# A new order of all queues, and eight PSUM banks shared by attention and MLP

## The chip, the cores and the metric

The kernel is one launch on one core of a Trainium2 chip. The core has engines that work side by side, each through a queue of its own, in the order in which the program gives it its instructions: TensorE (PE; the loading of its weights is listed as PEld), VectorE (DVE), ScalarE (ACT) and GpSimd (POOL). SyncE (SP) issues the DMA transfers in this kernel. An instruction starts when those before it on its engine are done and everything that it reads is there; until then all behind it on that engine stands too. TensorE writes to PSUM, which has eight banks of 2 KB for each of 128 partitions.

The metric is the time of the whole launch in microseconds (us). Three runs of the kernel before took 535.52, 535.54 and 535.78; the median is 535.54.

## What is computed

A recurrent attention, followed by an MLP with a hard-swish:

```python
state = zeros((B, H, D, D))                     # B, H, S, D = 4, 8, 768, 48
for t in range(S):
    state = alpha[:, :, t, :, None] * state + einsum('bhd,bhe->bhde', k[:, :, t], v[:, :, t])
    y[:, :, t] = einsum('bhd,bhde->bhe', q[:, :, t], state)
x = y.transpose(0, 2, 1, 3).reshape(B * S, H * D)     # 3072 x 384
h = x @ w_in                                          # 3072 x 2048
g = h * clip(h + 3, 0, 6) / 6
out = g @ w_out                                       # 3072 x 384
```

q, k, v and alpha come as 32-bit floats, the two weights as 64-bit floats. [...]

## The kernel before

**Tiling.** The tokens are cut into 24 *chunks* of 128, j = 0 to 23: six to each of the four batches, so chunks 0, 6, 12 and 18 begin with an empty state. Two chunks make a *group* of 256 tokens, g = 0 to 11, for the MLP.

**An order written by hand.** All work is cut into steps. A step is a function of the kernel, and the program is one string of 1788 words, each a step's short name and its numbers with dots between: `sc.3.1.3` is the scores of chunk 3 with PSUM tiles 1 and 3. `run` (L745 to L748) calls them one after the other inside `tc.manual_schedule()` (L750). A step may hold instructions for one engine or for several; each engine gets its instructions in the order of the string, and so does SyncE its DMAs. The string therefore sets the order of every queue at once, and which PSUM tile a step writes. Waits between engines follow from the data.

**Weights: 16 slices** of 768 KB, i = 0 to 7 of `w_in` and 8 to 15 of `w_out`. `w.i` loads a slice. `d1.i` (L186) and `d2.i` (L196) are ScalarE's passes over it, `dx.i` (L191) one more for slices 0, 1, 2 and 4; `d3.i` is VectorE's part, two instructions for those four slices (L203 and L205, a "half-size" weight) and three for the others (L207, L208 and L210, a "whole" one); `d4.i` (L217) is an addition on GpSimd that finishes the slice. A matmul on a slice needs its `d4`.

**Attention, for a chunk j.**
- `la`, `lk`, `lq`, `lv` load alpha, k, q and v (L251 and L262, L272). For the first six chunks alpha, k and q are transposed on TensorE (`ta`, `tk`, `tq`: four transposes each, L282, into one PSUM tile); for later ones on VectorE (L286).
- `ca` (L300) copies alpha's transpose to SBUF on ScalarE. `r` is a scan over the chunk on VectorE (L309) and a reciprocal, the decay; `p` (L320) a second scan, the growth. `k` and `q` (L332) multiply k by the one and q by the other, on VectorE.
- `sc` (L346) makes the scores on TensorE, in two PSUM tiles, `m` (L356) masks them on VectorE, four instructions. `qa.j.b` (L366) copies half of q beside the masked scores on ScalarE.
- k by token: `kb` (TensorE, L374) and `ck` (ScalarE, L378) for the first eight chunks; later `kt` (VectorE, L391), `kw` and `kr`, a way through DRAM.
- the state: `st` (L409) decays it on GpSimd, `sv.j.b` (L419; L415 at a batch's start) copies it beside v on ScalarE, `u` (L429) makes the update on TensorE, `sm.j.b` (L437, L439) adds it to the state on VectorE.
- `ya` and `yb` (L455) are the matmuls of the output of the first and second half of the chunk; `cy` (L464) copies the result to SBUF on ScalarE, as x of the MLP.

**MLP.** Groups 0 and 1 make the first layer with plain matmuls: `f` (L478), 12 matmuls for two of the 16 blocks of 128 hidden units; `fa` and `fb` (L489) do the same for the two chunks of group 0 apart. `fr` (ScalarE, L494) and `fg` (VectorE, L498) are the gate. Group 0 makes the second layer with plain matmuls too (`b`, L516, `bo`, `so`).

From group 2 on the first layer is a fast matrix product with 20 sub-products: `y` (VectorE, L537 to L541) makes sums of the blocks of `w_in` once, `xc.g` makes sums of a group's x, `M.g.i` (L600) is sub-product i, four matmuls, `n` (L606) keeps a result on ScalarE, `o` (L537 to L541) combines results on VectorE, `e` (L494) and `h` (L498) are the gate. From group 1 on the second layer has seven sub-products: `x` (L647) makes sums of `w_out` once, `s` (L647, L664) sums of the hidden units on VectorE, `P.g.i` (L703) is sub-product i, eight matmuls of which the profile has 16 records, `K` (L682) keeps a result on ScalarE, `G` (L719, and L716 on ScalarE) finishes a quarter of the output and `O` (L724) stores it.

**Pads.** `z.m.n` (L532) is n matmuls of the identity into a PSUM tile that nobody reads. The profile has two records for each.

**PSUM.** Two lists of four tiles, each tile one bank: `banks`, tiles t0 to t3, for attention's steps (`ta`, `tk`, `tq`, `kb`, `sc`, `u`, `ya`), and `bank_m`, tiles m0 to m3, for those of the MLP and the pads. A number in a word is an index in its list. A step that writes a tile waits until the last reader of what the tile held is done.

```python
banks = [ps.tile([C, NP * C], FP, tag=f"t{i}", name=f"t{i}_ps") for i in range(4)]        # L222
bank_m = [ps.tile([C, GT * 2], FP, tag=f"m{i}", name=f"m{i}_ps") for i in range(4)]       # L470
```

Of the kernel before, what the change touches and what calls it, by code (L numbers as in the profile page):

```python
# [17 lines left out]
def kernel(  # L18
# [42 lines left out]
    G = 2  # L61
# [161 lines left out]
    banks = [ps.tile([C, NP * C], FP, tag=f"t{i}", name=f"t{i}_ps") for i in range(4)]  # L223
# [246 lines left out]
    bank_m = [ps.tile([C, GT * 2], FP, tag=f"m{i}", name=f"m{i}_ps") for i in range(4)]  # L470

# [278 lines left out]
    with tc.manual_schedule():  # L750
        run("""z.0.5 z.0.3 z.0.1 z.0.8 qa.0.0 w.0 d2.0 d3.0 la.0 ta.0.0 ca.0 r.0 lk.0 tk.0.1 k.0
               z.0.2 p.0 la.1 ta.1.2 lq.0 tq.0.3 ca.1 r.1 lk.1 lv.0.0 sv.0.0 d1.0 kb.0.0 ck.0 z.0.2
               u.0.2.1 sm.0.0 sv.0.1 q.0 qa.0.1 tk.1.0 k.1 p.1 z.0.2 sc.0.2.3 m.0 la.2 ta.2.0 ca.2
               dx.0 w.2 d2.2 kb.1.0 ck.1 lq.1 r.2 sm.0.1 st.1 tq.1.2 q.1 d3.2 z.0.3 d1.2 dx.2 lv.1.1
               u.1.3.1 sv.1.0 sm.1.0 p.2 sm.1.1 sc.1.0.2 m.1 ya.0.3 yb.0 cy.0 lq.2 w.1 d1.1 tq.2.1
               q.2 d4.2 lk.2 tk.2.3 k.2 fa.2.0 d4.0 st.2 sc.2.0.2 d2.1 d3.1 m.2 dx.1 d4.1 qa.1.1
               lk.3 la.3 ta.3.1 ca.3 la.4 fa.0.1 sv.1.1 w.3 r.3 ta.4.3 ca.4 r.4 tk.3.1 k.3 kb.2.0
               qa.1.0 d2.3 ya.1.2 yb.1 cy.1 fa.1.2 lq.3 ck.2 d1.3 p.3 d3.3 lv.2.2 u.2.3.2 sm.2.0
               d4.3 fb.2 tq.3.1 q.3 fb.1 qa.2.0 sm.2.1 sv.2.0 st.3 fr.0.2.0 fg.0.2 lk.4 tk.4.0
               sv.2.1 w.5 d2.5 k.4 d3.5 d1.5 qa.3.0 d4.5 qa.2.1 sc.3.1.3 m.3 w.6 d2.6 d1.6 d3.6 d4.6  # L760
               lv.3.0 lq.4 w.7 kb.3.2 fb.0 f.0.3.3 kb.4.0 ya.2.1 ck.3 u.3.3.2 sm.3.0 fr.0.3.1 fg.0.3
               fr.0.1.0 fg.0.1 qa.3.1 sv.3.0 sm.3.1 p.4 d2.7 sv.3.1 d1.7 d3.7 d4.7 f.0.5.0 fr.0.5.1
               fr.0.0.0 fg.0.5 fg.0.0 tq.4.3 ck.4 la.5 ta.5.2 f.0.6.3 ca.5 w.4 d2.4 ya.3.0 yb.3 cy.3
               fr.0.6.1 yb.2 cy.2 w.9 d2.9 q.4 qa.4.1 d1.4 d1.9 dx.4 la.6 w.8 d3.4 r.5 lk.5 w.10
               d3.9 p.5 ca.6 fg.0.6 d4.9 w.12 lq.5 lv.4.1 d2.8 d3.8 f.0.7.2 d1.8 st.4 d4.8 d4.4 w.11
               fr.0.7.0 fg.0.7 f.1.7.0 fr.1.7.1 fg.1.7 sc.4.0.2 m.4 f.1.1.1 fr.1.1.0 fg.1.1 f.1.3.3
               fr.1.3.1 d2.10 d1.10 tk.5.3 f.1.0.2 d2.12 d3.10 d4.10 w.13 fg.1.3 fr.1.0.0 fg.1.0 k.5
               d3.12 lq.6 f.1.6.0 f.1.2.1 u.4.1.0 sm.4.0 d1.12 d4.12 sv.4.0 qa.4.0 ya.4.2 fr.1.6.1
               fg.1.6 w.15 tq.5.3 fa.4.3 sv.4.1 d2.11 kb.5.1 d2.13 fr.1.2.0 f.1.4.2 fr.1.4.1 d1.11
               sm.4.1 q.5 r.6 d3.11 d3.13 fg.1.4 d4.11 lv.5.0 lk.6 tq.6 p.6 d2.15 d3.15 fg.1.2 d1.13  # L770
               d4.13 sc.5.0.3 yb.4 f.1.5.0 fr.1.5.1 fg.1.5 tk.6 m.5 b.1.0.2 fb.4 b.1.1 d1.15 d4.15
               st.5 y.5 w.14 la.7 lk.7 cy.4 d2.14 qa.5.1 ck.5 b.0.0.1 fr.0.4.0 d3.14 k.6 q.6 ca.7
               fg.0.4 d1.14 d4.14 x.0 y.1 y.10 b.0.1 y.0 y.2 u.5.2 P.1.0.0 K.1.0 qa.5.0 sv.5.0
               qa.6.1 P.1.1.3 b.0.2 b.1.2 kb.6.0 ya.5.3 y.6 s.1.0.0 sm.5.0 sv.5.1 G.1.0.0 tk.7
               s.1.1.1 s.1.2.3 x.1 yb.5 cy.5 b.1.3 sc.6.1.2 lv.6.2 ck.6 u.6.3.0 s.1.3.2 x.2 P.1.2
               b.0.3 K.1.1 y.7 s.1.4 s.1.5 y.11 y.3 r.7 xc.2.1 x.3 y.4 y.8 xc.2.3 k.7 xc.2.0 xc.2.4
               y.9 y.12 y.16 y.13 y.15 P.1.3.3 K.1.2 P.1.4 bo.1 P.1.5 xc.2.5 G.1.1.1 P.1.6 y.14 y.17
               y.19 xc.2.6 sm.6.0 G.1.2.2 y.20 M.2.0.2 lv.12.1 la.8 O.1.1 O.1.0 ca.8 y.18 y.21 y.23
               so.1 G.1.3.3 n.2.0.8 bo.0 lq.7 lv.7.0 O.1.2 m.6 xc.2.2 xc.2.10 xc.2.7 tq.7 r.8 p.7
               xc.2.8 sv.6.1 M.2.15.3 M.2.1 kb.7.3 n.2.1.9 M.2.16 M.2.2 n.2.2.10 M.2.7.0 n.2.7.11  # L780
               sm.6.1 xc.2.9 q.7 p.8 M.2.3 M.2.4 n.2.4.12 M.2.8 o.2.0.0 M.2.5 n.2.5.13 qa.7.0 sv.6.0
               st.7 lk.8 O.1.3 lq.8 lk.9 la.9 la.10 tk.8 tq.8 lq.10 lq.9 ya.6.1 yb.6 M.2.9 z.1.3
               M.2.18.1 o.2.1.0 e.2.1.1 M.2.10 cy.6 ck.7 sc.7.0.2 u.7.1.3 n.2.10.14 M.2.11 qa.7.1
               ca.9 la.11 y.22 M.2.6.2 h.2.1 q.8 m.7 e.2.0.0 h.2.0 n.2.11.15 qa.6.0 n.2.18.10 qa.8.1
               M.2.12 M.2.19 n.2.12.12 M.2.13 sm.7.0 sv.7.1 r.9 k.8 o.2.3.0 sv.7.0 ya.7.0 y.24
               o.2.5.0 n.2.13.12 o.2.2.0 yb.7 cy.7 sc.8.1.2 xc.3.1 o.2.2.1 e.2.2.1 xc.3.3 o.2.3.1
               M.2.14 xc.3.4 xc.3.0 xc.3.5 o.2.4.0 xc.3.7 xc.3.6 o.2.6.0 P.2.0.1 M.3.0.2 M.2.17
               h.2.2 o.2.6.1 e.2.3.0 h.2.3 o.2.7.0 K.2.0 n.3.0.12 M.3.1 n.3.1.9 e.2.5.1 M.3.7.0
               n.3.7.13 xc.3.8 o.2.7.1 xc.3.2 kt.8 e.2.6.0 h.2.6 tk.9 M.3.2 n.3.2.10 e.2.4.0 P.2.1.3
               h.2.4 h.2.5 s.2.0.14 e.2.7.0 G.2.0.1 h.2.7 M.3.3 M.3.4 n.3.4.8 k.9 s.2.1.11 M.3.8  # L790
               o.3.0.0 ca.10 kt.9 P.2.3.3 s.2.2.15 s.2.3.14 lv.8.2 kw.8 kr.8 lk.10 sm.7.1 xc.3.9
               M.3.5 n.3.5.11 K.2.2 e.3.0.1 xc.3.10 M.3.9 o.3.1.0 P.2.2 K.2.1 u.8.0.3 M.3.18.2 s.2.5
               M.3.10 n.3.10.14 n.3.18.15 e.3.1.0 s.2.4 P.2.4 tq.9 h.3.0 st.8 sv.8.0 M.3.11 n.3.11.8
               tk.10 p.9 sm.8.0 q.9 r.10 k.10 qa.9.0 qa.9.1 m.8 sm.8.1 h.3.1 M.3.19 o.3.5.0 kt.10
               P.2.5 G.2.2.0 st.9 M.3.12 sc.9.0.1 qa.8.0 n.3.12.10 o.3.3.0 kw.9 lv.9.0 kr.9 sv.8.1
               u.9.2.3 sm.9.0 sv.9.1 sv.9.0 G.2.1.2 sm.9.1 st.10 M.3.15.2 M.3.16 M.3.6.3 M.3.13 m.9
               o.3.4.0 o.3.6.0 tq.10 n.3.13.10 o.3.2.0 e.3.4.1 ya.8.2 yb.8 ya.9.3 yb.9 cy.9 M.3.14
               M.3.17 cy.8 xc.4.1 P.2.6 e.3.5.0 G.2.3.3 o.3.2.1 xc.4.3 h.3.4 xc.4.4 o.3.6.1 xc.4.5
               xc.4.0 xc.4.6 e.3.2.1 M.4.0.0 n.4.0.10 P.3.0.1 xc.4.7 o.3.7.0 p.10 h.3.5 o.3.3.1
               xc.4.8 M.4.7.3 M.4.1 xc.4.2 h.3.2 o.3.7.1 lk.11 O.2.2 tk.11 e.3.6.0 e.3.3.1 h.3.3  # L800
               P.3.1.2 e.3.7.1 n.4.1.13 M.4.2 K.3.0 ca.11 q.10 h.3.6 r.11 k.11 h.3.7 n.4.7.15
               lv.10.2 lv.11.0 kw.10 sc.10.0.1 kr.10 G.3.0.0 u.10.3.2 sm.10.0 qa.10.1 n.4.2.14 M.4.3
               M.4.4 M.4.8 s.3.0.9 xc.4.9 s.3.2.12 s.3.1.11 P.3.3.2 n.4.4.8 M.4.5 o.4.0.0 e.4.0.0
               sv.10.1 sm.10.1 xc.4.10 kt.11 O.2.0 O.2.3 lq.11 m.10 s.3.3.9 s.3.5 M.4.9 o.4.1.0
               P.3.2 sv.10.0 st.11 n.4.5.11 K.3.2 la.13 M.4.18.0 p.11 tq.11 lk.12 tk.12 K.3.1 M.4.10
               n.4.10.9 q.11 qa.10.0 n.4.18.12 e.4.1.1 la.12 s.3.4 ca.12 h.4.0 r.12 P.3.5 G.3.2.1
               h.4.1 M.4.11 P.3.4 n.4.11.8 M.4.12 n.4.12.14 qa.11.0 M.4.19 p.12 G.3.1.3 lq.12 kw.11
               O.2.1 tq.12 kr.11 u.11.3 sc.11.0.2 sv.11.0 O.3.1 lk.13 P.3.6 qa.11.1 M.4.6.2 G.3.3.2
               k.12 o.4.3.0 m.11 sm.11.0 sv.11.1 kt.12 M.4.13 n.4.13.14 q.12 o.4.3.1 e.4.3.0 o.4.2.0
# [123 lines left out]
```

## Time and profile before

| | us |
|---|---|
| median of three runs | 535.54 |
| span of the profiled execution, first to last instruction | 533.7 |
| TensorE busy in the first 38 us | 32.04 |
| TensorE busy from 38 to 80 us | 42.00 |
| TensorE busy from 80 to 130 us | 49.71 of 50 |
| TensorE busy from 130 to 480 us | 350.00 of 350 |
| TensorE busy in the last 54 us | 50.82 |
| VectorE busy in the same five stretches | 32.81, 39.76, 49.57, 327.85, 27.25 |
| ScalarE busy, whole span | 257.2 |
| GpSimd busy, whole span (none after 480) | 50.4 |

How to read the profile. A line of a group gives the source line, the engine, the operation, output and inputs by the program's names, the shape and the number of instructions, then the busy time, the mean of one in ns, and behind the second bar the idle time of the engine just before them, with what ended most of it. `m_ps` and `t_ps` stand for the tiles m0 to m3 and t0 to t3. The chain of waits is followed back from the last instruction: each line is a stretch of work (start, length, engine, operation, line) that ended just before the next could start. In the timeline a row begins with its start and its length. Matmuls overlap, and a busy time of TensorE counts the time in which at least one record is open, so "busy" is not "at its peak". The granted clock of TensorE is 1.00 in every stretch of this profile.

### The profile page before, as it was taken

Reading aid. Unit: us, or ns where it says so; the run is one execution under the profiler, and the core shown is the slowest. Engines: PE = TensorE matmul, PEld = TensorE weight load, DVE = VectorE, ACT = ScalarE, POOL = GpSimd, SP = SyncE. Lnnn points to the kernel's source line nnn. Section 1 sums busy time; section 2 is a strip of 40 time slices with the busy share of each in tenths; the row PEclk is TensorE's granted clock in tenths of the full one; section 3 lists DMA queues with packets and bytes.
Section 4 is the critical chain, followed back from the end, with each engine's and each line's share of the span. In section 5 each row is a group of like instructions: output and inputs, shape, how many; then the busy total and the mean of one; then the engine's idle time right before and its main releaser. Section 6 shows DMA issues by size and latency. Waiting matters only on the chain.

```text
span 533.7 us, 15143 instructions
## 1 busy us (share of the span) xinstructions
PE 524.6 (98%) x6306; PEld 499.4 (94%) x6306; DVE 477.2 (89%) x849; ACT 257.2 (48%) x503; POOL 50.4 (9%) x71
## 2 busy tenths in 40 slices
PE   8799999999999999999999999999999999999997
PEld 7698886789999999999999999999999999999997
DVE  6999989999999999998999999999999899496382
ACT  3889865212653553553544444642634544553340
POOL 5333425100000000000000000000000000000000
DMA  9998876005615155254344355044454042100001
GB/s 174 217 252 256 215 216 152 21 2 154 152 30 116 32 121 135 57 140 95 87 110 113 91 124 140 19 120 102 115 136 104 11 110 43 44 2 2 15 16 37
DMA packets 124100, 54.40 MB, mean 102 GB/s; under 512 B 83328, under 2 KB 116864, under 8 KB 124032
## 3 DMA queue, kind: packets, MB, share of 16 engines
q1 hardware_dynamic: 124032, 53.44, 42.5%
q8 instruction: 49, 0.80, 0.6%
q14 instruction: 19, 0.16, 0.1%
HBM read 44.50 MB, written 8.91 MB: 100 GB/s over the span
## 4 chain that ended last, share of the span: by engine, by line
PE 85%; DVE 8%; POOL 2%; DMA 2%; ACT 1%; issue 1%; SPq 1%; DVEq 0%; POOLq 0%
PE m_ps L703 34%; PE m_ps L600 34%; PE m_ps L478 5%; PE t_ps L455 4%; PE t_ps L346 2%; PE t_ps L429 2%; PE m_ps L489 2%; PE t_ps L282 1%; DVE rings L647 1%; DMA v<-in_v_dram 1%; DVE raw L537 1%; ACT raw L191 1%; DMA kq<-in_k_dram 1%; DVE g_sb L647 1%; DVE w L537 1%
## 5 line engine op out<-in xcount | busy, mean ns | idle before, releaser
L606 ACT COPY g_sb<-m_ps 128x512 f32<-128x512 f32 x110 | 63.6, 584 | 124.9 <-PE m_ps L600 104.1
L703 PE MATMUL m_ps<-w,g_sb 128*128 128x192 f32 x704 | 121.7, 327 | 0.0
L703 PEld LDWEIGHTS m_ps<-w,g_sb 128*128 128x128 f32 x704 | 113.7, 190 | 0.4
L703 PE MATMUL m_ps<-rings,g_sb 128*128 128x192 f32 x528 | 91.5, 326 | 0.0
L703 PEld LDWEIGHTS m_ps<-rings,g_sb 128*128 128x128 f32 x528 | 85.4, 190 | 0.1
L600 PE MATMUL m_ps<-xc,w 128*128 128x128 f32 x640 | 82.7, 277 | 0.3 <-DVE w L541 0.3
L600 PEld LDWEIGHTS m_ps<-xc,w 128*128 128x128 f32 x640 | 77.5, 192 | 1.5 <-issue 0.5
L494 ACT ACTIVATE r<-g_sb,half 128x512 f32<-128x512 f32 x80 | 56.8, 722 | 32.9 <-DVE g_sb L541 12.1
L498 DVE SCALAR_TENSOR_TENSOR g_sb<-r,g_sb 128x512 f32<-128x512 f32 x80 | 53.6, 682 | 4.6 <-ACT r L494 4.2
L600 PE MATMUL m_ps<-xT,raw 128*128 128x128 f32 x400 | 52.5, 277 | 0.0
L600 PEld LDWEIGHTS m_ps<-xT,raw 128*128 128x128 f32 x400 | 48.6, 192 | 0.6
L409 POOL TENSOR_TENSOR st<-sm,R 128x192 f32<-128x192 f32 x20 | 12.9, 643 | 353.8 <-DVE sm L439 306.7
L647 DVE TENSOR_TENSOR g_sb<-g_sb 128x512 f32<-128x512 f32 (+1 forms) x55 | 42.0, 795 | 0.2
L600 PE MATMUL m_ps<-xT,w 128*128 128x128 f32 x320 | 42.0, 276 | 0.0
L600 PEld LDWEIGHTS m_ps<-xT,w 128*128 128x128 f32 x320 | 39.3, 192 | 0.1
L366 ACT COPY A<-q 48x256 f32<-48x256 f32 x88 | 35.5, 404 | 5.0 <-DVE q L332 3.7
L356 DVE TENSOR_TENSOR A<-t_ps,mask 64x256 f32<-64x256 f32 x96 | 36.0, 414 | 0.4
L478 PE MATMUL m_ps<-xT,w 128*128 128x256 f32 x144 | 32.8, 382 | 0.0
L600 PE MATMUL m_ps<-xc,raw 128*128 128x128 f32 x240 | 31.8, 276 | 0.0
L309 DVE TENSOR_TENSOR_SCAN R<-t,ones 128x516 f32<-128x516 f32 x24 | 29.7, 1236 | 1.1 <-ACT t L300 1.0
L478 PEld LDWEIGHTS m_ps<-xT,w 128*128 128x128 f32 x144 | 26.7, 190 | 3.6
L600 PEld LDWEIGHTS m_ps<-xc,raw 128*128 128x128 f32 x240 | 29.6, 192 | 0.1
(104 smaller groups left out, 731.0 us busy)
## 6 DMA issues: line engine op xcount, KB each, us to landing
raw<-in_moe_w_out_dram SPq DMA_DIRECT2D x8, 768.0 KB, 5.2
raw<-in_moe_w_in_dram SPq DMA_DIRECT2D x6, 768.0 KB, 6.8
v<-in_v_dram SPq DMA_DIRECT2D x48, 96.0 KB, 3.0
out_dram<-oh SPq DMA_DIRECT2D x44, 96.0 KB, 1.7
far<-kq SPq DMA_DIRECT2D x64, 64.0 KB, 2.2
kb<-far SPq DMA_DIRECT2D x64, 64.0 KB, 2.0
aq<-in_alpha_dram SPq DMA_DIRECT2D x36, 96.0 KB, 2.5
qq<-in_q_dram SPq DMA_DIRECT2D x36, 96.0 KB, 2.4
```

The lines of the kernel that those rows point to most:

```text
L309: nc.vector.tensor_tensor_scan(out=reverse(R, n - 1, n), data0=reverse(ax, n, n), data1=reverse(ones, n, n), initial=0.0, op0=ALU.mult, op ...
L356: nc.vector.tensor_tensor(out=to[:, a], in0=sc[a][half], in1=mask[half, half].unsqueeze(1).to_broadcast([HB, NP, HB]), op=ALU.mult)
L366: nc.scalar.copy(out=to[:, a], in_=Q_t[j][64 * a : 64 * a + D, :, half])
L409: nc.gpsimd.tensor_tensor(out=st, in0=sm, in1=R_t[j][:, :, 0:1].to_broadcast([C, NP, D]), op=ALU.mult)
L455: nc.tensor.matmul(y_of(j, (i + 1) // 2, p)[:, HB * b : HB * b + HB], vb[:, p, e : e + 32], A_t[j][:, b, 2 * p + a], start=(b == 0 and i = ...
L478: nc.tensor.matmul(h[:, f], w1[:, kk, o : o + C], xT_t[g][:, kk], start=(kk == 0), stop=(kk == KT - 1))
L494: nc.scalar.activation(out=to, in_=h, func=AF.Relu, bias=half, scale=1.0 / 6.0)
L498: nc.vector.scalar_tensor_tensor(out=to, in0=r, scalar=1.0, in1=h, op0=ALU.min, op1=ALU.mult)
L600: nc.tensor.matmul(acc[g][i][:, f * C : (f + 1) * C], spots[w][:, f * C : (f + 1) * C], x_of(g, x), start=(first and f == 0), stop=last, s ...
L606: nc.scalar.copy(out=slots[z], in_=acc[g][i])
L647: nc.vector.tensor_tensor(out=out, in0=in0, in1=in1, op=ALU.subtract)
L703: nc.tensor.matmul(to[g], a, rhs[:, f], start=(first and f == 0), stop=(last and f == HF - 1), skip_group_check=True)
```

## The change

One line is added behind L470 (so lines below it have a number higher by one in the kernel after), and the string is another one. The steps in it are the same: the same chunks, slices and sub-products, and 29 pad matmuls. What differs is where each stands, and the last numbers of a word, which name a PSUM tile, one of the tiles for v, or a place where a result is kept.

With the added line both lists have all eight tiles, in a different order: index 0 to 3 is what it was, and index 4 to 7 is a tile of the other list. A step of attention may now write where the MLP wrote, and the other way round.

```diff
     bank_m = [ps.tile([C, GT * 2], FP, tag=f"m{i}", name=f"m{i}_ps") for i in range(4)]
+    banks, bank_m = banks + bank_m, bank_m + banks
...
     with tc.manual_schedule():
-        run("""z.0.5 z.0.3 z.0.1 z.0.8 qa.0.0 w.0 d2.0 d3.0 la.0 ta.0.0 ca.0 r.0 lk.0 tk.0.1 k.0
-               z.0.2 p.0 la.1 ta.1.2 lq.0 tq.0.3 ca.1 r.1 lk.1 lv.0.0 sv.0.0 d1.0 kb.0.0 ck.0 z.0.2
...
-               lv.3.0 lq.4 w.7 kb.3.2 fb.0 f.0.3.3 kb.4.0 ya.2.1 ck.3 u.3.3.2 sm.3.0 fr.0.3.1 fg.0.3
...
-               st.5 y.5 w.14 la.7 lk.7 cy.4 d2.14 qa.5.1 ck.5 b.0.0.1 fr.0.4.0 d3.14 k.6 q.6 ca.7
-               fg.0.4 d1.14 d4.14 x.0 y.1 y.10 b.0.1 y.0 y.2 u.5.2 P.1.0.0 K.1.0 qa.5.0 sv.5.0
...
-               st.7 lk.8 O.1.3 lq.8 lk.9 la.9 la.10 tk.8 tq.8 lq.10 lq.9 ya.6.1 yb.6 M.2.9 z.1.3
...
-               G.11.1.0 P.11.5 G.11.2.1 O.11.2 P.11.6 G.11.3.2 O.11.1 O.9.2 O.11.3""")
+        run("""z.5.2 z.7.8 la.0 ta.0.5 z.0.3 ca.0 r.0 lq.0 tq.0.4 p.0 q.0 la.1 z.3.3 ta.1.7 ca.1
+               lk.0 tk.0.6 z.1.2 k.0 kb.0.0 w.0 sc.0.1.3 ck.0 lk.1 tk.1.5 z.3.1 lv.0.0 qa.0.1
...
+               lv.3.0 sc.3.1.4 qa.2.0 fa.2.6 qa.3.0 fb.2 m.3 r.4 st.3 u.3.1.4 p.4 sv.2.1 sm.3.0
+               tk.5.6 lq.4 tk.4.5 k.4 sv.3.0 ya.2.0 fr.0.2.0 yb.2 cy.2 sm.3.1 la.5 tq.4.7 q.4
+               ta.5.1 st.4 sv.3.1 w.6 ya.3.4 yb.3 qa.4.1 cy.3 d1.6 d2.6 sc.4.5.7 w.5 m.4 kb.4.3
+               qa.4.0 d3.6 f.1.0.4 f.1.2.0 w.3 ck.4 fg.0.2 d2.5 d1.5 d3.5 ca.5 la.7 d2.3 d3.3
...
+               p.6 qa.6.0 cy.5 xc.2.1 xc.2.3 q.6 w.13 d2.13 xc.2.0 lv.7.1 d1.15 xc.2.4 d3.13 xc.2.5
+               w.14 d2.14 lk.8 d3.14 K.1.0 d4.15 y.3 y.5 xc.2.7 y.6 b.0.0.4 s.1.1.1 sv.6.1 b.0.1
+               d1.14 lq.8 qa.6.1 d4.14 s.1.0.0 y.0 xc.2.6 M.2.7.6 lv.8.0 y.1 y.2 d1.13 d4.13 x.0
...
+               sm.7.1 M.2.9 o.2.1.0 k.8 kt.8 kw.8 ya.6.7 e.2.1.1 h.2.1 y.22 yb.6 lv.9.2 tq.8 cy.6
...
+               P.11.2 K.11.1 P.11.3.7 P.11.4 K.11.2 P.11.5 O.11.0 G.11.1.0 O.11.1 G.11.2.2 O.11.2
+               P.11.6 G.11.3.1 O.11.3""")
```

On SyncE's queue the first loads were w.0, la.0, lk.0, la.1, lq.0, lk.1, then v of chunk 0; they are la.0, lq.0, la.1, lk.0, w.0, lk.1, then v of chunk 0. In front of the first transposes of alpha stood 17 pads, and now stand 10. The string of the kernel after ends with the last store of group 11 alone; before it, the string had a store of group 9 among its last three words.

## The prediction

> **What bounds it now.** I read the page's busy shares and slices first, then who waits on TensorE, then the last chain, then the timeline of the start.
>
> ```profile
> PE 524.6 (98%) x6306; PEld 499.4 (94%) x6306; DVE 477.2 (89%) x849; ACT 257.2 (48%) x503; POOL 50.4 (9%) x71
> ...
> DVE  6999989999999999998999999999999899496382
> ```
>
> TensorE is busy for 98% of the span, VectorE (DVE) for 89%, and in tenths VectorE is full from the second slice on. Busy TensorE is no proof of pace, so the waits and the chain:
>
> ```profile
> PE m_ps L532 <- POOL ident masks.py:199: 1.5, 1, 1.5
> PE t_ps L429 <- issue: 1.2, 2, 1.0
> PE t_ps L455 <- DVE s L439: 0.7, 1, 0.7
> ...
> PE m_ps L600 <- DVE w L541: 0.3, 1, 0.3
> ```
>
> TensorE's waits come to some 6 us in all, and the last is 0.3 us at 128 us, on a weight sum of VectorE. The chain's end shows the pace of the rest:
>
> ```profile
> 501.98 6.25 PE m_ps L600 x56
> 508.23 2.60 PE m_ps L703 x16
> 510.84 1.78 PE m_ps L600 x16
> 512.62 18.22 PE m_ps L703 x112
> ...
> 530.86 0.32 ACT oh L716
> ```
>
> 16 records of L703 (one P step) take 2.60 us, 16 of L600 (two M steps) 1.78, with nothing between them. So I price TensorE's queue by steps: P 2.60, M 0.89; from other pieces of the chain f 2.59, fa and fb 1.34, four transposes 0.44, one of sc, ya, yb or u some 0.45 to 0.48; a b step 2.60 (8 records between their starts). Both orders hold the same steps, 504 us of them. The span is 533.7; so 30 us are not work, and only they can change. I call "lost" a step's start less the work queued before it.
>
> ```profile
> 1.46 6.75 PE L532 MATMUL m_ps<-ident 128*128 128x128 f32 x34 [1.46 <-POOL ident masks.py:199]
> ...
> 8.05 1.04 PE L282 MATMUL t_ps<-ident,rings 128*128 128x128 f32 x8
> ...
> 8.93 0.61 PE L532 MATMUL m_ps<-ident 128*128 128x128 f32 x4
> ...
> 9.31 1.23 DVE L309 TENSOR_TENSOR_SCAN R<-t,ones 128x516 f32<-128x516 f32 x1 [1.02 <-ACT t L300]
> ```
>
> The first transposes of alpha start at 8.05, directly behind 34 pad records that took 6.6 us; later 4 pads take 0.45. When chunk 3's scores start, at 37.73, the queue holds 24.8 us before them (26 pad steps 5.8, 17 groups of transposes 7.6, 5 fa/fb 6.7, 10 of u, sc, ya, yb 4.7): 12.9 lost. The M step with the wait at 128.04 has 111.6 before it: 16.4 lost. The last P starts at 528.06 with 501.5 before it: 26.6 lost. So half of the loss falls in the first 38 us. Most of the rest is a change of matmul kind: going from a large kind to a small one costs 93 ns in the median, back 134.
>
> **The change, step by step.** Sums are against the profiled span 533.7; the median of the runs, 535.54, is 1.9 longer, and I carry that over.
>
> *Eight shared banks.* No wait on TensorE above is for a bank after the first 31 us. Freed work cannot be faster than dense work: 0 by itself. It only lets steps stand in another order. The Trainium skill (Perfetto Trace Analysis, Matmul Optimizations) tells readers to make use of all eight banks; before does use all eight, in two sets of four, and no later wait here speaks for a gain.
>
> *Start.* Alpha's load goes from second on SyncE's queue to first, the 768 KB weight slice w.0 from first to fifth, behind alpha, q, alpha and k; the leading pads fall from 34 records to 20, at 0.22 us each (6.6 over 34, with the faster last ones), which end at about 5.9. Alpha's load is issued near 0.75; bounds for its landing are 2.5 us (median of the 96 KB alpha loads) and 5.6 (the 192 KB ones of the crowded first 40 us): 3.3 to 6.4. I take it as covered by the pads. Then four transposes to 6.8, ScalarE's copy (0.58) to 7.5, and the first scan at 7.5 (8.0 by the late landing) against 9.31. But before has by then converted w.0 on VectorE (1.41), which after must do later: net gain on VectorE's clock 0.4 (0 to 0.5).
>
> *Chunk 3.* From the first scan through q.3 VectorE has, at start to start paces (decay scan and reciprocal 1.24, growth scan 1.14, multiply 0.60, masked 4 x 0.34, state sum 0.27, half-size weight 1.41, whole one 2.04), in before 27.2 us with w.0: 5 decays, 4 growths, 8 multiplies, 3 masks, 5 sums, 3 halves and 1 whole, 1 gate. It ends at 37.6, a lag of 10.4, or 2.5 more than the 7.9 at the start. After has 4 decays, 4 growths, 8 multiplies, 3 masks, 4 sums, 3 halves, 1 gate: 24.3. With a lag of 7.5 + 2.5 = 10.0, q.3 ends at 34.3 and the scores start at 34.45 with 23.0 us of TensorE work before them: 11.4 lost, 1.5 less than before.
>
> *A new wait.* After q.4 VectorE comes to d3.6 with only a mask step (1.36) between. d3.6 waits for ScalarE, whose queue has qa.4.1 (0.66), cy.3 (0.38), d1.6 (0.81), d2.6 (0.93) behind q.4, with hand-overs 3.1 us. VectorE stands 1.8 (bounds 0, if those copies are early, and 3.1). Behind d3.6 are two gates and d3.5, d3.3, and the f steps wait for them. In return, before's wait of 1.28 at 72.6 (state sum of chunk 4 for its update matmuls) should go, since update 4 now stands a whole f step ahead: -1.3 (0 at worst). Net +0.5.
>
> *GpSimd.* The sixteen d4 additions move against VectorE's work. In the trace two of them stretch a VectorE step:
>
> ```profile
> 81.81 2.02 POOL L217 TENSOR_TENSOR w<-raw 128x768 int32<-128x768 int32 x1 [0.17 <-POOL kq L257]
> ...
> 92.51 1.69 POOL L217 TENSOR_TENSOR w<-raw 128x768 int32<-128x768 int32 x1 [3.76 <-DVE raw L210]
> ```
> ```profile
> 82.47 1.78 DVE L207 TENSOR_SCALAR w<-w 128x768 f32<-128x768 f32 x1
> ...
> 92.80 1.95 DVE L332 TENSOR_TENSOR q<-q,P 128x512 f32<-128x512 f32 x1
> ```
>
> L207 elsewhere takes 0.55, L332 0.68: 1.25 lost each, until the GpSimd step ended. The Trainium skill (Perfetto Trace Analysis, Optimizing Scalar/DVE Operations) says that the two share a read port which a two-port VectorE step locks; by it, d4.13 to d4.15, which in after stand among q.6 and the weight sums y, all from SBUF, would hit three times, an estimate of 3.8 from the rows above. Most d4 in before (14 of 16) cost nothing of that size. Bounds: no hit (-2.5) to five (+3.8). I take between one and two, -0.7.
>
> *The products of group 2.* M.2.9 has 120.2 us of VectorE before it in after and 120.8 of TensorE (hand-over included); before's nearest places stand 0.4 to 0.6 the other way round, too. So TensorE's loss there is VectorE's lag less 0.6. Lag in before 17.0 at y.23, and 17.7 at the kept sum o.2.0; after -0.4 +0.5 -0.7 = 0.6 less. With 0.1 for the place: 0.5 gained. TensorE's own line (1.5 gained at chunk 3) isn't the later one here, so 1.0 of it is given back.
>
> *The rest.* From group 3 on VectorE's work lies further ahead of its users than before (group 2's third P: 0.8 behind in before, 0.9 ahead in after), so I see TensorE dense to the end: 0.2 gained. Between steps of different kind there are 109 switches before and 100 after (scores and updates stand in runs): by 93 and 134 ns and 23 between scores and updates, 10.8 against 10.5 us: 0.4 gained. Pads are 29 steps in both. The last M has P.10.6 and P.11.1 behind it, 5.2 us, over the 3.7 of sum, gate, product and two sums on ScalarE and VectorE: covered; store and landing unchanged. The DMA queue's order is covered by the start's row.
>
> Sum: -0.5 -0.2 -0.4 = -1.1: span 532.6, time 534.4.
>
> The skill's page TensorE: Matmul & The Clock Gate (Part 1) says that a window of idleness halves the clock again. With fewer pads in front that would speak against the change. The trace shows the pads' pace going from 222 ns (19 in 4.2 us) to 112 and no return, with gaps up to 1 us; the sum keeps 112, and by the rule a lost window of 3.4 us would cost up to 1.7.
>
> **Rivals.** *No change:* the wait at d3.6 isn't made good and hits stay at two: lag -0.4 +1.8 -1.3 = +0.1, 0.2 given at the place, and 0.6 from the rest: 535.0 (534.5 to 536.5 with the bounds). For it: the orders meet VectorE at the same place. Here the change doesn't do what it says: the banks are of no account.
> *Slower:* GpSimd's additions hit VectorE's SBUF steps four or five times between 75 and 105 us. Two more than before: +2.5 on the lag, from +1.7 (535.5 + 1.1) on it counts as slower: with the terms above and 0.6 off, 537.0. For it: the y sums all read SBUF; against it: 14 harmless additions.
> *More:* no hits, no wait at d3.6: TensorE's own line sets the end, 1.5 + 0.6 + 0.7 (small waits before 128): 532.7.
>
> **How the numbers follow.** Forecast 0.40, no change 0.25, slower 0.25, more 0.10. A measurement of this kernel tells about 0.2%, 1.07 us, from none: under 534.47 is faster. Of the forecast's own range, 533.4 to 535.3, a bit over two thirds counts as faster; with all of the last rival and a little of the second that makes 0.42; same 0.33; slower 0.25. Eight times in ten: 532.7 to 537.0.
>
> **What would show it.** First scan near 7.5 us; chunk 3's scores near 34.5; a wait of d3.6 on ScalarE's d2.6 near 43; stretched L207, L332 or L537 beside L217; at M.2.9 a loss of 16; TensorE dense from 130 us. Wrong: the first scan after 8.5, waits of TensorE past 150 us, or a slower pad pace after 8 us.

## The result: 2.9% slower

| | before | after |
|---|---|---|
| median of the runs, us | 535.66 (535.52 to 535.92, 4 runs) | 551.25 (549.63 to 552.93, 4 runs) |
| ratio, with its 95% interval | | 1.029 (1.0267 to 1.0312) |
| span of the profiled execution | 533.7 | 550.0 (a run of 551.76) |

The forecast was 534.4, with 532.7 to 537.0 as its range. The change costs 15.6 us, and the side was wrong too.

The page of the kernel after: busy time and share, then VectorE's busy tenths and TensorE's granted clock in 40 slices.

```profile
PE 529.0 (96%) x6306; PEld 501.3 (91%) x6306; DVE 492.1 (89%) x849; ACT 258.4 (47%) x503; POOL 54.0 (10%) x71
...
DVE  6996999999999999999999999999899999686481
...
PEclk9999998999999999999999999999999999999999
```

VectorE is busy for 492.1 us instead of 477.2 with the same 849 instructions. Busy counts the time in which at least one is open; the lengths of the 849 added up rise by less, from 534.2 to 540.4 us, so a few last longer, and the others overlap less with their neighbours. VectorE has a thinner fourth slice, and the page has a clock row with a slice under nine tenths, which the page before had not.

The list of what TensorE waited for (total us, times, longest) has new entries at its head, and its first two name no releaser:

```profile
PE m_ps L346 <- issue: 2.9, 1, 2.9
PE m_ps L429 <- issue: 2.2, 1, 2.2
PE t_ps L282 <- DVE g_sb L499: 2.0, 1, 2.0
...
PE t_ps L601 <- DVE xc L538: 1.1, 1, 1.1
...
PE t_ps L479 <- POOL w L217: 1.1, 1, 1.1
PE t_ps L704 <- DVE rings L648: 0.8, 1, 0.8
```

To see where 16.3 us of span went, take the prediction's measure again: "lost" is a TensorE step's start less the work queued before it, at the same paces for both orders. Beside it stands the same for VectorE, its "lag": a step's end less VectorE's work up to it.

| at | lost before | lost after | VectorE's lag before | after |
|---|---|---|---|---|
| scores of chunk 3 (q.3 for VectorE) | 12.9 | 11.4 | 10.4 | 10.1 |
| M.2.9 (o.2.0.0 for VectorE) | 16.8 | 28.7 | 17.7 | 29.5 |
| the last P | 26.6 | 42.9 | | |

So three stretches: the start gained 1.5 us, from there to M.2.9 (149.5 us) 13.4 were lost, and from M.2.9 to the end another 4.4. At M.2.9 the loss is VectorE's lag less 0.8 in the kernel after and 0.9 in the one before. In the kernel after TensorE stands there for VectorE's sum o.2.0.0, as one more line of its list has it:

```profile
PE t_ps L601 <- DVE g_sb L538: 0.2, 1, 0.2
```

So what has delayed VectorE up to there comes out as TensorE's loss. In the kernel before, M.2.9 starts 0.08 us behind that sum too, but directly behind other matmuls, without a wait.

### Two places where VectorE fell behind

The first is at 42 us. VectorE's timeline in the kernel after (start, length, instruction, in brackets the idle time before it and what ended it):

```profile
41.28 0.69 DVE L332 TENSOR_TENSOR q<-m_ps,P 128x512 f32<-128x512 f32 x1 [0.16 <-PE m_ps L282]
46.58 1.53 DVE L356 TENSOR_TENSOR A<-m_ps,mask 64x256 f32<-64x256 f32 x4 [4.61 <-PE m_ps L346]
```

and TensorE's at the same place:

```profile
42.64 0.44 PE L346 MATMUL m_ps<-q,k 48*64 48x64 f32 x10
45.97 0.57 PE L346 MATMUL m_ps<-q,k 48*64 48x64 f32 x22 [2.89 <-issue]
```

The masking m.4 stood for 4.6 us, since the scores sc.4 stopped after 10 of their 32 records, inside a step, where nothing that it reads can be late.

The second is spread from 50 to 109 us: GpSimd's additions d4, which add the low bits of a weight to its high ones, and VectorE's steps beside them. GpSimd's timeline, then VectorE's:

```profile
50.79 1.46 POOL L217 TENSOR_TENSOR w<-raw 128x768 int32<-128x768 int32 x1 [8.60 <-ACT w L196]
...
99.28 1.48 POOL L217 TENSOR_TENSOR w<-raw 128x768 int32<-128x768 int32 x1 [5.43 <-ACT raw L186]
105.62 3.67 POOL L217 TENSOR_TENSOR w<-raw 128x768 int32<-128x768 int32 x2 [4.86 <-DVE raw L210]
```
```profile
51.19 1.61 DVE L207 TENSOR_SCALAR w<-w 128x768 f32<-128x768 f32 x1
...
54.44 0.68 DVE L207 TENSOR_SCALAR w<-w 128x768 f32<-128x768 f32 x1
55.16 1.58 DVE L208 TENSOR_SCALAR w<-w 128x768 uint32<-128x768 uint32 x1
...
99.35 1.56 DVE L538 TENSOR_TENSOR xc<-xT 128x128 f32<-128x128 f32 x1
...
106.00 1.96 DVE L542 SCALAR_TENSOR_TENSOR raw<-w 128x512 f32<-128x512 f32 x1
107.88 1.55 DVE L538 TENSOR_TENSOR xc<-xc 128x128 f32<-128x128 f32 x1
```

An xc sum takes 0.29 elsewhere and 1.55 here, the weight sum y.5 0.69 and 1.96 here: each 1.27 longer, until the GpSimd instruction beside it had ended. The lines at 54 and 55 us stand beside an addition that runs from 54.66 to 56.19: L207, begun 0.22 before it, kept its length, and L208, begun inside it, did not.

### The profile page after: what moved, and what is told of

It reads as the page before. It is cut to its first block, busy times and chain, and to the rows that moved or that the text cites. A ratio compares the mean times of both kernels' runs of the same rounds, so it can differ in the third digit from the quotient of the medians.

```text
span 550.0 us, 15090 instructions
## 1 busy us (share of the span) xinstructions
PE 529.0 (96%) x6306; PEld 501.3 (91%) x6306; DVE 492.1 (89%) x849; ACT 258.4 (47%) x503; POOL 54.0 (10%) x71
## 4 chain that ended last, share of the span: by engine, by line
PE 52%; DVE 26%; SPq 3%; issue 3%; DMA 3%; ACT 1%; DVEq 0%; ACTq 0%
PE t_ps L704 15%; PE m_ps L601 12%; PE t_ps L601 11%; PE m_ps L704 9%; SPq L262 3%; DVE g_sb L499 2%; DVE g_sb L648 2%; DMA aq<-in_alpha_dram 2%; PE m_ps L455 2%; DVE A L356 2%; DVE k L286 1%; DVE P L320 1%; DVE g_sb L538 1%; DVE t L286 1%; DVE R L309 1%
## 5 line engine op out<-in xcount | busy, mean ns | idle before, releaser
L704 PE MATMUL t_ps<-w,g_sb 128*128 128x192 f32 x496 | 86.0, 327 | 0.0
L704 PEld LDWEIGHTS t_ps<-w,g_sb 128*128 128x128 f32 x496 | 80.2, 190 | 0.6 <-DVE s L439 0.2
L704 PE MATMUL t_ps<-rings,g_sb 128*128 128x192 f32 x336 | 58.4, 327 | 0.8 <-DVE rings L648 0.8
L704 PEld LDWEIGHTS t_ps<-rings,g_sb 128*128 128x128 f32 x336 | 54.4, 190 | 1.2 <-DVE rings L648 1.0
L601 PE MATMUL m_ps<-xc,w 128*128 128x128 f32 x336 | 44.8, 278 | 1.0 <-issue 0.6
L601 PE MATMUL t_ps<-xc,w 128*128 128x128 f32 x304 | 40.4, 279 | 1.8 <-DVE xc L538 1.1
L704 PE MATMUL m_ps<-w,g_sb 128*128 128x192 f32 x208 | 36.1, 327 | 0.0
L704 PEld LDWEIGHTS m_ps<-w,g_sb 128*128 128x128 f32 x208 | 33.7, 190 | 0.1
L704 PE MATMUL m_ps<-rings,g_sb 128*128 128x192 f32 x192 | 33.3, 327 | 0.0
L309 DVE TENSOR_TENSOR_SCAN R<-t,ones 128x516 f32<-128x516 f32 x24 | 29.6, 1232 | 3.7 <-ACT t L300 3.4
L704 PEld LDWEIGHTS m_ps<-rings,g_sb 128*128 128x128 f32 x192 | 31.0, 190 | 0.1
L320 DVE TENSOR_TENSOR_SCAN P<-t 128x516 f32<-128x516 f32 x24 | 29.8, 1243 | 0.3
```

The costliest lines, as they stand in the source:

```text
L309: nc.vector.tensor_tensor_scan(out=reverse(R, n - 1, n), data0=reverse(ax, n, n), data1=reverse(ones, n, n), initial=0.0, op0=ALU.mult, op ...
L320: nc.vector.tensor_tensor_scan(out=P_t[j], data0=aX[j % 2][:, 0:n], data1=ini[j % 2], initial=0.0, op0=ALU.mult, op1=ALU.add)
L601: nc.tensor.matmul(acc[g][i][:, f * C : (f + 1) * C], spots[w][:, f * C : (f + 1) * C], x_of(g, x), start=(first and f == 0), stop=last, s ...
L704: nc.tensor.matmul(to[g], a, rhs[:, f], start=(first and f == 0), stop=(last and f == HF - 1), skip_group_check=True)
```

## The experiments

"V" is the theory that VectorE's lag sets the end; "B" that the shared banks' own waits are the cost; "F" that TensorE's stops without a releaser are the loading of its code.

### The scores of chunk 4 first

```diff
-               ... tq.4.7 q.4
-               ta.5.1 st.4 ... d1.6 d2.6 sc.4.5.7 w.5 m.4
+               ... tq.4.7 q.4 sc.4.5.7
+               ta.5.1 st.4 ... d1.6 d2.6 w.5 m.4
```

> The order after, with sc.4 moved up to directly behind q.4. Theory V: VectorE's own queue sets the end, and what made the order after slower is VectorE's lag (28.2 us at 150 us against 18.0 before), of which 4.8 come from the stand at m.4 (46.6 us), because TensorE stopped for 2.9 us inside sc.4. With sc.4 in front, m.4 starts by 43 us and the lag falls by 3 to 4: the time falls by 3 to 4.5 us against the kernel after, 547 to 548. TensorE's stop without a releaser stays near its instruction number 1473 and falls into the attend matmuls of chunk 3, if it is the loading of its code; if it is sc.4's own data, it moves with sc.4. Theory B: the two waits for a shared bank (tq.5, u.6) are the cost: the time stays within 1 us of 551.

551.47 (551.20 to 554.70; 1.0309, 1.0279 to 1.0339): no gain, where theory V had promised 3 to 4.5 us. m.4 did start at 42.3 instead of 46.6. TensorE's, ScalarE's and VectorE's timelines of this kernel show what came of it:

```profile
42.73 0.88 PE L455 MATMUL m_ps<-A,v 128*32 128x64 f32 x43
46.28 0.53 PE L455 MATMUL m_ps<-A,v 128*32 128x64 f32 x21 [2.67 <-issue]
```
```profile
46.90 0.48 ACT L464 COPY xT<-m_ps 128x384 f32<-128x384 f32 x1 [4.20 <-PE m_ps L455]
47.40 0.91 ACT L186 ACTIVATE raw<-raw 128x768 int32<-128x768 uint32 x1
48.21 0.87 ACT L196 ACTIVATE w<-raw 128x768 f32<-128x768 f32 x1
```
```profile
49.11 0.69 DVE L207 TENSOR_SCALAR w<-w 128x768 f32<-128x768 f32 x1 [5.31 <-ACT w L196]
```

The stop did not move with the scores. It stayed at TensorE's instruction 1473 (matmuls, weight loads and the waits on TensorE's own queue, counted in order of start) and now cut the attend of chunk 3. ScalarE's cy.3 waited for that attend, d1.6 and d2.6 stood behind cy.3, and VectorE's d3.6 waited 5.3 us for d2.6. This is the wait that the prediction named, with another cause and three times the size. A stall was passed to VectorE by another way.

### Loads held back

```diff
-               qa.4.0 d3.6 f.1.0.4 f.1.2.0 w.3 ck.4 fg.0.2 d2.5 d1.5 d3.5 ca.5 la.7 d2.3 d3.3
+               qa.4.0 d3.6 f.1.0.4 f.1.2.0 lv.4.0 w.3 ck.4 fg.0.2 d2.5 d1.5 d3.5 ca.5 la.7 d2.3 d3.3
...
-               fr.1.0.0 lv.4.0 fg.1.6 ...
+               fr.1.0.0 fg.1.6 ...
```

> The order after, with lv.4.0 moved up to directly ahead of w.3: SyncE then waits for the attend of chunk 3 (about 42 us) before it issues w.3, alpha of chunk 7 and w.4, which it issued from 33 to 37 us. Theory F: TensorE's stop inside sc.4 is a block of its own code (16 KB) whose load stood in the DMA queues behind data that took 10.7 us to land; with 1.5 MB less in the queues the load starts by 40 instead of 43.0 us, TensorE's stop shrinks from 2.9 to 1 us or less, VectorE's stand at m.4 from 4.6 to 2, its lag at 150 us by 2.5 to 3, and the time falls by 2 to 3.5 us, to 548 to 549.5. If the stop has another cause, it stays at 2.9 and the time within 1 us of 551; if d3.3 then has to wait for w.3, up to 2 us of the gain are given back.

549.09 (548.53 to 550.67; 1.0262, 1.0246 to 1.0277), 2.2 us off the kernel after by the medians; the two intervals still touch, so the time alone is weak evidence, and the trace has to show the cause. w.3 is now issued at 43.3 us instead of 33.5. TensorE runs through sc.4, and VectorE stands 1.4 instead of 4.6 us:

```profile
42.28 0.69 PE L346 MATMUL m_ps<-q,k 48*64 48x64 f32 x32
```
```profile
43.03 1.53 DVE L356 TENSOR_TENSOR A<-m_ps,mask 64x256 f32<-64x256 f32 x4 [1.42 <-PE m_ps L346]
```

The page lists an instruction queue, q8, with 49 packets and 0.80 MB, which is 16 KB for each; TensorE's 12,719 instructions (12,612 matmuls and weight loads and 107 on its queue) are 49.7 times 256. Worked out from the trace's records of these packets and of TensorE's instructions (a block is 256 of them, taken to begin at number 193 over a multiple of 256; TensorE's stand is counted from start to start, which adds 0.2 to 0.3 to the wait in its list; us):

```
                block  used up in   its successor's load starts / lands   TensorE stands
                                    (from the block's begin)              at its end
before            20      2.3         -1.8 / -0.9                            0.0
before            24      2.8         -2.3 / -1.3                            0.0
after              4      3.1         +3.2 / +4.6                            3.1
after             24      3.2         +1.8 / +2.7                            0.8
after             36      2.2         +0.6 / +1.5                            0.8
loads held back    4      3.0          0.0 / +1.1                            0.0
```

Inside a step TensorE stopped with no releaser, in the kernels with the order after, at numbers 1473, 6593 and 9665: 193 over a multiple of 256 each time. (The other entry "issue", at L429, is another matter, below.) The profiles have 25 such stops, and in all of them TensorE went on 1.2 to 1.7 us after that packet had landed; in none of the 16 profiles did it enter a block sooner than 1.2 us after its packet. Attend, scores and update steps are 64 instructions of 7 ns each; four or five of them in a row use up a block in 2 to 3 us. The order before has such rows as well, but in the two of the table the load had landed before the block was begun. At 43 us four weight slices and alpha of two chunks had been issued within 7 us and took up to 10.8 us to land; the code landed among them. Theory F holds.

The Trainium skill (Runtime: NRT & Kernel Launch, Instruction fetch mechanics) says that code comes in blocks of 16 KiB, 256 instructions, and that this is mostly hidden, since instructions are issued more slowly than blocks arrive. The block size agrees with the trace; the hiding does not: the list of waits has stops of 0.2 to 4.2 us where a dense block met a late load.

### Scores first, and ScalarE's order

```diff
-               ta.5.1 st.4 sv.3.1 w.6 ya.3.4 yb.3 qa.4.1 cy.3 d1.6 d2.6 sc.4.5.7 w.5 m.4 kb.4.3
+               ta.5.1 st.4 sv.3.1 w.6 d1.6 d2.6 ya.3.4 yb.3 qa.4.1 cy.3 w.5 m.4 kb.4.3
```

with sc.4 behind q.4 as above.

> The order after with sc.4 directly behind q.4, and d1.6 and d2.6 on ScalarE ahead of the copies that wait for the attend of chunk 3 (in the run with sc.4 alone moved, d3.6 waited 5.3 us for d2.6, which stood behind cy.3). Theory V: TensorE's stop of 3 us stays, but VectorE no longer meets it; its lag at 150 us falls by 4 (28.2 to 24), the time by 3 to 4.5 us, to 546.5 to 548. If TensorE's own stops set the end, the time stays within 1 us of 551.

548.71 (547.44 to 550.62; 1.0248, 1.0228 to 1.0267): 2.5 us off, a little under the forecast. TensorE's stop of 2.4 us stays, m.4 and d3.6 no longer wait, but d3.5 then waits 2.5 us for d2.5, which still stands behind cy.3; the lag at o.2.0.0 is 27.0. So the time that TensorE's stop costs depends on how much of it VectorE meets.

### Other banks

```diff
-tq.5.1 ... f.0.6.2 ... f.0.7.5 ... u.6.7.1
+tq.5.6 ... f.0.6.5 ... f.0.7.2 ... u.6.0.1
```

> The order after, with four bank numbers changed, so that neither tq.5 nor u.6 writes a bank that a gate of VectorE has still to read (tq.5.6, f.0.6.5, f.0.7.2, u.6.0.1). Theory B (shared banks are the cost): the waits of 2.2 at 65.5 us and 2.4 at 92.6 us go, and with the second the stretch at half clock (1.8): the time falls by 4 to 6 us, to 545 to 547. Theory V (VectorE's lag): the waits go, but TensorE waits as long for VectorE a little later; the lag at 150 us stays at 28, the time falls by 0 to 1 us, to 550 to 551.

551.34 (550.30 to 554.61; 1.029, 1.0272 to 1.0307): no change. In the kernel after the waits were real. The update u.6 has its data by 89.6 us, but its bank holds the plain product f.1.4, which VectorE's gate fg.1.4 has still to read; TensorE starts 0.1 us after that gate, and the list calls it "issue". Lines of the timeline, and TensorE's windows with the granted clock in the column ahead of the DMA share:

```profile
91.80 0.69 DVE L499 SCALAR_TENSOR_TENSOR g_sb<-r,m_ps 128x512 f32<-128x512 f32 x1
...
92.59 0.31 PE L429 MATMUL m_ps<-v,kb 64*64 64x48 f32 x1 [2.21 <-issue]
```
```profile
88.00:92.00 4.00, 2.36 (x131) 1.00 0.86 224
92.00:96.00 4.00, 3.41 (x36) 0.57 1.07 331
```

After the idle 2.2 us the clock was granted by half for 3.4 us, and the update and the b step behind it took 4.8 us, against 3.3 in the kernel with the other banks, where this wait and the half clock behind it are gone. This is what stands first in the list of that kernel:

```profile
PE t_ps L601 <- DVE xc L538: 5.6, 1, 5.6
```

The time saved at 92 us is spent at 110 us on the same late VectorE, with a half clock of 3.4 us behind that wait. The waits for banks were a sign of its lag, not a cause. Theory B falls, for the order as it is.

### Without GpSimd's additions

```diff
-        "d1": round_low, "d2": magnitude, "dx": sign, "d3": high_bits, "d4": add_low,
+        "d1": round_low, "d2": magnitude, "dx": sign, "d3": high_bits, "d4": lambda i: None,
```

> The order after without the sixteen d4 additions on GpSimd (the weights then lack their low bits). Theory V with GpSimd's part: about 8 us of stretched VectorE instructions go, and with them as much of the lag at 150 us (28 to 20 or 21): the time falls by 6 to 9 us, to 542 to 545. If the additions are of no account, it falls by less than 1 us.

> The order before without the sixteen d4 additions on GpSimd (the weights then lack their low bits). Theory V: before has 3 us of stretched VectorE instructions, so the time falls by 1.5 to 3 us, to 532.5 to 534, a third of the fall in the order after. If the fall is as large as in the order after, GpSimd does not tell the two orders apart.

After: 541.74 (541.02 to 542.99; 1.0116, 1.0099 to 1.0134), 9.5 us less, a little over the forecast. Before: 534.87 (534.63 to 535.20; 0.9986, 0.9977 to 0.9995), less by 0.5 to 0.8, and the forecast of 1.5 to 3 was missed. The loss at M.2.9 falls from 28.7 to 19.0 in the one and from 16.8 to 16.0 in the other. The sixteen additions are the same in both kernels; what they meet is not: the VectorE instructions beside them are stretched by 8.0 us in all after and by 3.1 before. Why 3.1 us cost so little in the order before is not shown. Nor do the 8.0 us make up the 9.5 alone: taking out the additions also takes out TensorE's waits for their results (1.1 us at L479 in its list above). The next run has only three additions taken out.

```diff
-        ... "d4": add_low,
+        ... "d4": lambda i: None if i >= 13 else add_low(i),
```

> The order after without d4.13, d4.14 and d4.15 alone (three weight slices then lack their low bits). In the order after these three met xc.2.0, y.5 and xc.2.7, which read SBUF alone, and stretched each by 1.27 us. Theory V: the lag at 150 us falls by 3.8, the time by 3 to 4 us, to 547.3 to 548.3. If VectorE's steps at 99 to 109 us are not on the path, the time stays within 1 us of 551.

547.32 (545.86 to 549.01; 1.0217, 1.0192 to 1.0242), 3.9 us less, for three additions that had stretched VectorE by 3 x 1.27 = 3.8. The same three steps of VectorE in this kernel:

```profile
97.89 0.29 DVE L538 TENSOR_TENSOR xc<-xT 128x128 f32<-128x128 f32 x1
...
103.74 0.69 DVE L542 SCALAR_TENSOR_TENSOR raw<-w 128x512 f32<-128x512 f32 x1
104.34 0.29 DVE L538 TENSOR_TENSOR xc<-xc 128x128 f32<-128x128 f32 x1
```

They are back at their usual lengths.

### The additions cut in pieces

```diff
-        nc.gpsimd.tensor_tensor(out=dst.bitcast(I32), in0=high.bitcast(I32),
-                                in1=lo.bitcast(I32), op=ALU.add)
+        for m in range(dst.shape[1]):
+            nc.gpsimd.tensor_tensor(out=dst[:, m].bitcast(I32), in0=high[:, m].bitcast(I32),
+                                    in1=lo[:, m].bitcast(I32), op=ALU.add)
```

> The order after, each d4 addition on GpSimd cut into three (first layer) or two (second layer) instructions. A stretched VectorE instruction lasted until the GpSimd addition that it met had ended, 1.27 us longer at most. If it is let in between two pieces, a hit costs 0.5 to 0.7 at most, the stretched time falls from 8 to 3 or 4 us, and the time by 4 to 5.5 us, to 545.5 to 547. If VectorE is held until all pieces are done, or is met by each piece anew, the time stays at 550 to 552.

> The order before with the same cut of the d4 additions. Without the additions it was 0.5 us faster, so the cut can bring 0.2 to 0.5 us: 534.9 to 535.3. If it met VectorE more often, 535.5 to 536.5.

After: 551.15 (549.52 to 552.20; 1.0288, 1.0271 to 1.0305), no gain. A hit costs 0.63 instead of 1.27, but six steps (xc, xc, y, xc, y, s) are hit instead of three, 3.8 us again: the next piece meets the next step. The profiled execution also had a stop of 4.2 us at instruction 1473, for which VectorE stood 6.3 at m.4 instead of 4.6. Before: 534.98 (534.62 to 535.52; 0.9988, 0.9979 to 0.9997), 0.6 us less, as much as without the additions.

### What is left

> The order after with the loads held back (lv.4.0 ahead of w.3) and without the sixteen d4 additions (the weights then lack their low bits). If the code load at 43 us (2.2 us of time in the run with the loads held back) and the additions (9.5 us in the run without them) are separate causes, they add up: 551.3 - 2.2 - 9.5 = 539.6, between 539 and 540.2. TensorE's loss at M.2.9 then is 17 (before: 17), and what is left against the order before without additions (534.9) is 4.7 us, all of it after 150 us. If they overlap, 540.5 to 542.

> The same with the four other bank numbers too (tq.5.6, f.0.6.5, f.0.7.2, u.6.0.1). With VectorE no longer late, theory B would show its own part: the wait of u.6 for a bank (1.4 us in the run without additions) goes, and the time falls by 1 to 1.5 us against the run without this edit. Theory V: M.2.9 waits for VectorE in any case, the time stays within 0.5 us of it.

Without the other banks: 541.78 (539.43 to 544.00; 1.0098, 1.0076 to 1.0119). This lies in the range for an overlap, not in that for a sum: by the medians, holding back the loads brought nothing on top of leaving out the additions. Its profiled execution, the slowest of the four (544.0), shows VectorE waiting 2.1 us for ScalarE's pass over a weight slice that landed late. With the other banks: 539.63 (539.18 to 541.30; 1.0078, 1.0063 to 1.0093). The intervals overlap, so whether the banks are worth something here, and whether code and additions add up, stays open. In the second kernel TensorE's loss at M.2.9 is 17.1, against 28.7 in the kernel after, and 16.0 in the order before without additions: code, additions and banks together account for what the order after lost up to there, but for 1.1. What is left is 4.8 us against the order before without additions.

Most of that rest is the tail. From M.2.9 to the last P the order before lost 9.8 or 9.9 us in all four of its kernels; the order after 13.2 to 14.4 in nine of the ten kernels so far that keep its steps there, however late they came to M.2.9. (The tenth, with the other banks alone, lost 16.7: its profiled execution was the slowest of its five, 554.61, with waits of its own at 288 us.) In the kernel after the trace puts 3.4 us of it down to 16 starts within 0.15 us of the end of a ScalarE or VectorE step that they needed (before: 0.4 at four), and 1.6 to stops at instructions 6593 and 9665; changes of matmul kind cost 1.1 less than before.

```diff
-... n.4.5.14 M.4.12 n.4.12.13 u.11.2 sc.11.7.5 M.4.13 sm.11.0 n.4.13.8 G.3.1.1 P.3.6 ...
+... n.4.5.14 u.11.2 M.4.12 n.4.12.13 sc.11.7.5 P.3.6 M.4.13 sm.11.0 n.4.13.8 G.3.1.1 ...
...
-e.8.1.0 m.18 u.19.7.1 ... ya.18.6 yb.18 lv.23.2 ya.19.0 yb.19 M.8.18.3 cy.18 q.20 la.22 P.7.4 ...
+e.8.1.0 m.18 P.7.4 u.19.7.1 ... ya.18.6 yb.18 lv.23.2 ya.19.0 yb.19 M.8.18.3 cy.18 q.20 la.22 ...
```

and three more, alike (P.5.0, M.6.5, P.6.5).

> The kernel of the run before (loads held back, other banks, no d4 additions: 539.6 us, its lowest 539.2) with five steps of TensorE moved after 150 us: P.3.6 and u.11 between M.4.11, M.4.12 and M.4.13, P.5.0 ahead of M.6.1, M.6.5 ahead of M.6.11, P.6.5 ahead of M.7.19, P.7.4 ahead of u.19 and the four attend steps. In that run TensorE waited there 0.50, 0.28, 0.24 and 0.21 us for copies of ScalarE that had only just begun, and stopped for 0.85 us at a multiple of 256 instructions in P.7.4 (code). If the rest of the difference to the order before is made of such waits, the time falls by 1.5 to 2.1 us, to 537.5 to 538.1. If VectorE or another line takes their place, it stays at 539.2 to 540.

> The order after with its whole computation (all d4 additions) and the three repairs together: loads held back, other banks, the five moved steps. From the run with the loads held back (549.1): 1.5 to 2 us for the moved steps, 0 to 2 for the banks: 545.5 to 547.5. If the additions' hold on VectorE makes the other repairs vain, 548.5 to 549.5.

545.09 (543.83 to 546.56; 1.0173, 1.0155 to 1.0191) and 553.54 (552.72 to 554.83; 1.0335, 1.032 to 1.0351): both slower, against their forecasts: by 5.5 us than the same kernel without the moved steps, and by 4.4 than the one with the loads held back. In the first, the stop at 9665 shrank from 0.8 to 0.1, as meant, but P.7.6 then waited 1.5 us for a sum of VectorE, M.7.12 0.7 for a copy and u.12 0.8 in two parts. Moving five steps by hand in a packed order opened more waits than it closed. Not all of the loss is theirs: between the profiled executions, 4.3 and 2.9 us of it fall behind M.2.9, but 1.2 and 3.4 ahead of it, where no step was moved. One of them also changes the result: P.6.5 ahead of K.6.2 puts its product into the sum that K.6.2 keeps, so group 6's output is another; the amount of work is the same. What the tail's 4.4 us would be worth to a better order is not shown.

### A version that is faster than both

The order before, with the additions cut, and with the start of the order after:

```diff
-        run("""z.0.5 z.0.3 z.0.1 z.0.8 qa.0.0 w.0 d2.0 d3.0 la.0 ta.0.0 ca.0 r.0 lk.0 tk.0.1 k.0
-               z.0.2 p.0 la.1 ta.1.2 ...
+        run("""z.0.5 z.0.3 z.0.1 z.0.2 qa.0.0 la.0 ta.0.0 z.0.6 ca.0 r.0 lk.0 w.0 d2.0 tk.0.1 k.0
+               z.0.2 p.0 d3.0 la.1 ta.1.2 ...
```

> The order before with the cut additions (534.98), and with the start of the order after: alpha's first load ahead of w.0, eleven pads instead of seventeen in front of the first transposes, six behind them, d3.0 behind the growth scan. The first scan then starts at 7.3 instead of 9.3 us, VectorE's work starts 0.6 later (before began with d3.0 at 6.6) but without its idle 1.0: 0.4 us gained on its lag. If that lasts to the end, 534.5 to 534.8; if TensorE's own line takes it back, 534.9 to 535.2; if the fewer pads leave a slower clock, over 535.5.

534.77 (534.24 to 535.45; 0.9983, 0.9974 to 0.9991): faster by 0.9 us, within 0.2%. The first scan starts at 7.45 instead of 9.31, and the loss at M.2.9 is 15.7, 0.6 below the run with the cut additions alone (16.3) and 1.1 below before. Against that run (534.98) the times alone do not separate.

## Why the prediction was wrong, step by step

*Banks, 0 by themselves:* right as far as was tried: two waits of 2 us for a bank came, and without them the time was the same.

*The start and chunk 3:* right. The first scan started at 7.6 (forecast 7.5), the scores of chunk 3 at 34.41 with 11.4 lost (34.45, 11.4). (The list for the order before names a gate that in fact stands behind q.3; its sum of 27.2 does not hold it.) The slower clock that the prediction weighed for fewer pads did not come in the profile of the kernel after: the pads ran at 213 ns up to 7.1 us in both kernels and at 111 from there. In the profiles of eight of the eleven kernels made from it, though, the clock was granted by half again from 11 to 13 us on, for 3.4 us (6.8 in one), behind a wait of 1.7 us at kb.0; seven of the eight still reached chunk 3's scores by 34.3 us.

*The new wait, +0.5:* right in its place to a few us, wrong in cause and size. VectorE stood 4.6 us at m.4, for scores of which the code had not come; without that, a wait of 5.3 at d3.6, where 1.8 had been priced. The working took TensorE to run whatever is queued once its data is there, and gave the loading of its code no term. The page's q8 row was there to be read; the "issue" entries before, 1.2 us, were no sign of it, since they do not stand at the end of a block. The promised gain, before's 1.28 at 72.6 us, did come.

*GpSimd, "between one and two, -0.7":* the step that failed most. Without the additions the order after is 9.5 us faster and the one before 0.5 to 0.8, so the term should have been about +9. The prediction had the Trainium skill's rule (Perfetto Trace Analysis, Optimizing Scalar/DVE Operations) before it, worked out three hits and 3.8 us from it for d4.13 to d4.15, and set it aside because 14 of 16 additions had been harmless. The trace shows these three hits, 3 x 1.27 = 3.8. What was harmless before is told by what it met: in the profiles of before, after, scores first and other banks 135 VectorE instructions ran beside an addition while reading PSUM (L332, L356, L439, L498), and none was stretched. Of those that read SBUF alone, the transposes of L286 (9) and the reciprocals of L313 (6) were not stretched either. For the others it mattered which began first: of 26 that began before the addition none was stretched, of 39 that began inside it 34 were, and the other five met only its last 0.13 to 0.24 us. Among the 34 are all sums xc and y of that kind, 13 of L207, one of L203, three of L208, the q.6 of before, and 7 scans (L309, L320), these by 0.4 only. The order after puts the additions among the weights' own d3, at 50 to 90 us, for 0.2 to 1.0 each, and among xc and y, for 1.27 each. So counting the places where SBUF readers begin inside an addition was the step to take; counting how many additions had been harmless was not.

*M.2.9, "loss is lag less 0.6":* right (0.8). That is why both errors reached M.2.9, and through it the end, and why the half clock at 92 us, 1.5 us on TensorE, need not have added to them.

*The rest, "dense to the end", 0.2 gained:* wrong, 4.4 lost, by small waits and two stops. The 0.4 for fewer changes of kind was 1.1.

*The rival "slower"* had the right mechanism, GpSimd, and 537.0 as its price (its own terms -0.4, +0.5, +2.5 and -0.6 make 537.5). Taken one by one the runs give 8.9 for the additions (9.5 less the 0.6 that they cost before), 2.2 for the code and 4.4 for the tail. That these come close to the 15.6 found is in part luck: the 1.5 gained at the start is not among them, and additions and code did not add up in the run that tried it. What is shown is that additions, code and banks together are the loss up to M.2.9; what the tail's share comes from is shown only in part.

## What to carry to other kernels

Before moving work on GpSimd, list for each of its long instructions which VectorE instructions will begin while it runs, and where these read: beside PSUM readers it was free here, and a sum from SBUF that began inside it lasted until it had ended. Count instructions as well as microseconds: a row of tiny matmuls can use up a block of code faster than a loaded DMA queue brings the next. And where one engine's lag sets a later meeting point, repairs on another engine only move the wait; look for what made the late engine late.

## What the runs showed of the hardware

TensorE's stops at the end of blocks of 256 instructions were not expected. The 16 KB packet of the next block began to move up to 3.2 us after the dense block was begun in the kernel after, and 4.9 in that with the cut additions, whose stops were 2.9 and 4.2 us. The runs of the order after spread over 3.3 us and the four of the order before over 0.4; that such stops make the spread is not shown.

The granted clock did not follow the length of a pause alone. In the kernel after it fell to 0.5 for 3.4 us after 2.2 us of idleness at 92 us, and stayed at 1.00 after the 2.9 at 43 us. In four other profiles (scores first, scores first with ScalarE's order, cut additions, three additions left out) the stop at 43 us was followed by 3.4 us of half clock, or 6.8 with the cut additions.
